# A ConvNeXt V2 block: PE drains replaced by waits, a narrower second read of yn, three more blocks stored whole, and reloads issued by SyncE

## The chip, the cores and the metric
The kernel runs on one core of one Trainium2 chip. The metric is device time in microseconds. Three runs of the kernel before took 1484.35, 1483.92 and 1483.01 us, a median of 1483.92. The engines are called PE (TensorE; PEld is its weight load), DVE (VectorE), ACT (ScalarE), POOL (GpSimd) and SP (SyncE, which here only issues transfers).

## The reference
The input x is one image of 512 x 512 pixels with 96 channels in bf16.

```python
out = sum of xp[:, i:i+H, j:j+W, :] * dw[i, j]      # 3 x 3 depthwise convolution
h = _layernorm(out, axis=-1)                        # over the 96 channels
h = gelu(einsum('bhwc,ce->bhwe', h, w1))            # 96 -> 384
gx = sqrt((h * h).sum(axis=(1, 2)) + 1e-6)          # over all pixels, one value per channel
nx = gx / (gx.mean(axis=-1) + 1e-6)
h = grn_gamma * (h * nx) + grn_beta + h
return x + einsum('bhwe,ec->bhwc', h, w2)           # 384 -> 96
```

The sum of squares over all pixels splits the work: no output can be made before every pixel has gone through the first product and gelu.

## The kernel before
The image is cut into 128 blocks of four rows (2048 pixels). A quad is 512 pixels of a block; a block has four. The program has two phases.

**Phase 1** makes the statistics, in slots of one block each (lines 831 to 955). A slot loads x (SP), transposes it (DVE, `turn_x`), convolves (PE, `conv_taps`, lines 462 to 504), takes the layer norm's moments, writes the normalized yn to memory and reads it again with channels on partitions (`stage_write`, `stage_read`), and for an older block runs the first product and gelu (`mlp_units`: nine ACT instructions that turn PSUM banks into g). Sums of squares of g are taken by DVE (`entry`, one statistics instruction of 512 columns per third of a quad) for as many quads as `cm_quads` says, and by PE (`gram_next`) for the rest. There are 14 slots without MLP: the ramp and a few after it; the last 14 blocks go through `mlp_tail`.

The convolution uses PE in row tiles: weights of 64 x 32, so that the upper 64 partitions (h = 0) and the lower 64 (h = 1) can work at once. It has three bursts of 24 matmuls; burst n gives the upper half bank n and the lower half bank n+1 (modulo 3). [...] 

**Phase 2** (lines 1003 to 1026) goes through the blocks in the order ORDER. For each block it needs g with channels on partitions, W2s (w2 with the statistics in it, made between the phases) and xb = x + bias. There are three kinds of block:
- *held* (5): g stayed in on-chip memory;
- *whole* (35, those with q % 10 in 0, 3, 7 below 114): g was stored in phase 1 in three pieces of 512 KB, one per slot (`store_next`), and is reloaded as `gl`, 1536 KB, into one of two buffers;
- *recomputed* (88): yn is read again (`ynT`, a ring of six buffers) and the first product and gelu are done again, quad by quad (`recompute`, `cm_unit`: three matmuls of 512 columns and one gelu of 1536). For three of them (KEPT) the last read of phase 1 is still there.

ORDER spreads held and whole blocks evenly among the recomputed ones. The schedule of the quads is written out: `pace` (line 371) issues recomputed quads between the four parts of a block's second product, evenly over phase 2 and at most five blocks ahead.

At each position n the loop loads what position n+5 needs (`load_rest`, line 284; `load_xr`, line 276, x for the residual, five buffers), lets POOL make xb of position n+2 (`stage_xb`, line 321, three buffers, each free when DVE has used it), runs the second product (`stage_mm2`, line 329: 48 matmuls of 96 columns into two PSUM banks, and four DVE instructions that add xb and write o_sb, four buffers) and stores the block before (`stage_out`, on SP).

For the order of work: up to position 7 the queues are used in program order (the wrapper `InOrder`); from position 8 on (FIRST = 8, line 1014) a scheduler orders each engine's instructions when the program is built, by when it thinks that they can start. Queues are in order on the chip: an instruction that waits holds back all behind it. POOL carries xr issues, gl issues and xb; SP carries ynT issues and stores.

The read of yn in phase 2 (line 295, `yn_rows`) takes 128 rows of 4 KB in one transfer: the 96 of block q and 32 of block q+1, which rows of zeros in w1p multiply.

Of the kernel before, what the change touches and what calls it, by code (L numbers as in the profile page):

```python
# [12 lines left out]
GR = 4  # L13
# [3 lines left out]
FILL = (6, 15)  # L17
BATCH = 4
NHELD = 5
WHOLE = (0, 3, 7)  # L20
NTAIL = 14
GRB = 3

# [33 lines left out]
def kernel(  # L57
# [13 lines left out]
    bf16 = x.dtype  # L71
    assert bf16 == mybir.dt.bfloat16

    B, H, W, C = x.shape
    E = w1.shape[1]
    assert B == 1 and dw.shape[0] == 3 and dw.shape[1] == 3
    assert C == 96 and E % 128 == 0 and W == 512
    NI = C // 32
    NCH = E // 128
    NG = W // 128  # L80
    NBLK = H // GR
# [5 lines left out]
    yn_dram = dram.tile([NBLK, C, GR * W], bf16, name="yn_dram")  # L87
    r_dram = dram.tile([NBLK, GR, W], bf16, name="r_dram")

    TAIL0 = NBLK - NTAIL  # L90
    HELD = [NBLK - 2 - 2 * i for i in range(NHELD)][::-1]
    KEPT = [NBLK - 5, NBLK - 3, NBLK - 1]
# [2 lines left out]
        return q in HELD  # L95

    def is_whole(q):
        return q < TAIL0 and q % 10 in WHOLE

    def cm_quads(q):  # L100
        if is_whole(q) or is_held(q):
            return NQ
        if q > HELD[0]:
            return 1
        return 2 if q >= NBLK - 16 or (q - 1) % 10 in WHOLE else 3

    whole = [q for q in range(NBLK) if is_whole(q)]
    g_dram = dram.tile([len(whole), 128, NQ * NCH * QW], bf16, name="g_dram")
# [10 lines left out]
    def quad_out(flat_ap):  # L119
        return flat_ap.rearrange("p (g r m) -> p g r m", r=GR, m=MB)  # L120

    def yn_src(q):
        return yn_dram[q].rearrange("c (r w) -> c r w", r=GR)

    def yn_rows(q):
        return yn_dram[q:q + 2].rearrange("q c (r w) -> (q c) r w", r=GR)[0:128]

    def yn_dst(q, r):
        return yn_dram[q].rearrange("(c i) (r w) -> r c i w", i=NI, r=GR)[r]

# [5 lines left out]
    dwx = consts.tile([9, NI, GR, 32], bf16, name="dwx")  # L136
    eye32 = consts.tile([128, 32], bf16, name="eye32")
    rowsel = consts.tile([128, GR], bf16, name="rowsel")
    w1_raw = consts.tile([C, E], bf16, name="w1_raw")
    w1p = consts.tile([128, E], bf16, name="w1p")  # L140
    Wq = consts.tile([128, NI, 3, GR, 32], bf16, name="Wq")
    w2_sb = consts.tile([128, NCH, C], bf16, name="w2_sb")
# [42 lines left out]
    with ExitStack() as p1:  # L185
# [98 lines left out]
        def load_rest(n, sq, pq):  # L284
            q = ORDER[n]
            v = grp.setdefault(q, {})
            if is_held(q):
                v["g"] = gs[q]
            elif is_whole(q):
                v["g"] = late.gl.tile([128, NQ, NCH, QW], bf16, name="gl")  # L290
                pq.dma_start(out=v["g"][:].rearrange("p t j w -> p (t j w)"), in_=g_dram[whole.index(q)])
            else:
                ynt = yn_ring[SLOTS[nth_made[q] % NYT]]
                if q not in KEPT:
                    sq.dma_start(out=ynt[:], in_=yn_rows(q))
                v["ynt"] = ynt

        def recompute(q, t):
            if t == 0:
                grp[q]["g"] = late.gr.tile([128, NQ, NCH, QW], bf16, name="gr")  # L300
            cm_unit(grp[q]["g"], grp[q]["ynt"], t)

        def cm_unit(g, ynt, t):
            U = banks3()
            for j in range(NCH):
                pe.matmul(quad_out(U[:, j, :]), lhsT=w1p[:, j * 128:(j + 1) * 128],
                          rhs=quad(ynt[:], t), start=True, stop=True)
            act.activation(out=g[:, t, :, :], in_=U, func=ACTF.Gelu_apprx_tanh)

# [116 lines left out]
        def setup_mlp():  # L426
            Us = banks(1)[:, 0, :]
            w1m, b2_ps = Us[:, :E], Us[:, E:E + C]
            pe.matmul(w1m, lhsT=cen[:], rhs=w1_raw[:], start=True, stop=True)
            for j in range(NCH):  # L430
                pe.matmul(b2_ps, lhsT=bet_bf[:, j:j + 1].to_broadcast([128, 128]), rhs=w2_sb[:, j, :],
                          start=(j == 0), stop=(j == NCH - 1))
            dve.scalar_tensor_tensor(out=w1p[:C, :], in0=w1m[:C], scalar=-1.0 / C, in1=w1_raw[:],
                                     op0=ALU.mult, op1=ALU.add)
            dve.tensor_copy(out=B2bc_f[:], in_=b2_ps)

        def setup_rest():
            dve.memset(ones_f[:], 1.0)
            dve.tensor_copy(out=gam[:], in_=gam_bf[:])

# [21 lines left out]
        def conv_taps(b, spare):  # L462
            if spare:
                Ua, Ub = banks(2), banks(1)
                Y = [Ua[:, 0, :], Ua[:, 1, :], Ub[:, 0, :]]
            else:
                Y = [Y3[:, i, :] for i in range(NI)]
            mms = []
            for n in range(3):
                mms.append([(h, j, (n + h) % NI, dx) for dx in (0, -1, 1) for j in range(GR) for h in range(2)])  # L470
            flat = [m for ms in mms for m in ms]
            first = {}
            last = {}
            for n, (h, j, i, dx) in enumerate(flat):
                first.setdefault((i, j), n)
                last[i, j] = n

            def burst(n, fence=True):
                k = sum(len(ms) for ms in mms[:n])
                for h, j, i, dx in mms[n]:  # L480
                    src = b + shift(h, j)
                    o0, o1 = max(0, -dx), W - max(0, dx)
                    pe.matmul(
                        Y[i][32 * j:32 * j + 32, o0:o1],
                        lhsT=Wq[64 * h:64 * h + 64, i, dx + 1, j, :],
                        rhs=x_rows(src, 64 * h, 64 * h + 64, i, MB * (1 + dx) + o0, o1 - o0)
                        if 0 <= src < NBLK else zrow[64 * h:64 * h + 64, o0:o1],
                        start=first[i, j] == k,
                        stop=last[i, j] == k,
                    )  # L490
                    k += 1
                if n < 2 and fence:
                    pe.drain()

            def evac():
                y = ypool.tile([128, NI, W], bf16, name="y_bf")
                if spare:
                    act.activation(out=y[:, 0:2, :], in_=Ua, func=ACTF.Identity)
                    act.activation(out=y[:, 2, :], in_=Ub[:, 0, :], func=ACTF.Identity)
                else:  # L500
                    act.activation(out=y[:], in_=Y3, func=ACTF.Identity)
                ybf[b] = y

            return [lambda fence=True, n=n: burst(n, fence) for n in range(3)], evac

        def stage_sq(b, on_act):
            q = ysqpool.tile([128, NI, W], bf16, name="ysq")
# [323 lines left out]
        for s in range(last_slot + 1):  # L831
# [30 lines left out]
            if mlp and mlp[0] >= TAIL0:  # L862
                assert not taps
                square_owed()
                mlp_tail(mlp[0], get)
            elif not mlp:
                if s + 3 < NBLK:
                    turn_x(s + 3)
                for f in taps:
                    f()  # L870
                if not spare:
                    spread_out()
                if evac:
                    evac()
                for b in get("sqa"):
                    stage_sq(b, True)
                for b in get("stats"):
                    stage_stats(b)
                for k in get("moments"):
                    stage_moments(k)  # L880
                if spare:
                    spread_out()
                for k in get("chain"):
                    stage_moments(k)
                    stage_chain(k)
                for k in get("turn"):
                    stage_turn(k)
                gram_next(2)
                square_owed()
            else:  # L890
                b = mlp[0]
                unit, squares, squares_rest = mlp_units(b)
                conv = lambda n, fence=True: taps[n](fence) if taps else None

                conv(0)
                unit(0, 2)
                unit(2, 1)
                squares(0)
                conv(1, False)
                spread_out()  # L900
                if s + 3 < NBLK:
                    turn_x(s + 3)
                unit(3, 1)
                unit(4, 2)
                squares(1)
                gram_next(1 if taps else 2)
                unit(6, 1)
                squares(2)
                unit(7, 1)
                for k in get("turn"):  # L910
                    stage_turn(k)
                conv(2)
                if evac:
                    evac()
                gram_next(1 if taps else 2)
                unit(8, 2)
                unit(10, 1)
                for b2 in get("stats"):
                    stage_stats(b2)
                unit(11, 1)  # L920
                for k in get("moments"):
                    stage_moments(k)
                squares_rest(2)
                square_owed()
                if is_whole(b):
                    owed.append(lambda f=squares_rest: f(3))
                grams.extend((b, c) for c in range(cm_quads(b) * QC, NQ * QC, 2 * E))
                if is_whole(b):
                    stores.extend((b, h) for h in range(3))
# [127 lines left out]
```

## Time and profile before

| | |
|---|---|
| runs, median | 1484.35, 1483.92, 1483.01 us; 1483.92 |
| span of the profiled execution | 1483.2 us (from the first to the last instruction; the page gives no other time for this execution, and the three runs take 0.2 us less to 1.1 us more than the span) |
| PE busy | 1392.2 us (94%) |
| ACT busy | 1415.9 us (95%) |
| POOL busy | 1300.7 us (88%) |
| DVE busy | 1166.9 us (79%) |
| bytes moved | 433.08 MB, 292 GB/s over the span; 410 to 415 in slices 31 to 35 of 40 |
| ACT g<-PS 128x1024, 128x512 | x342 of 1116 ns, x684 of 701 ns |
| ACT gr<-PS 128x1536 (recomputed) | x360 of 1455 ns |
| POOL xb<-xr 128x1536 | x118 of 3133 ns |
| POOL issues: xr, gl | 555 ns, 537 ns each |
| gl<-g_dram | x35, 1536 KB, 10.9 us from issue to landing |
| ynT<-yn_dram in phase 2 | x85, 512 KB each |
| out_dram<-o_sb | x127, 384 KB each |

A busy share is the time in which an engine has an instruction under way; successive instructions overlap a little, so a mean duration is longer than the distance between two starts, and distances between starts are what a bound engine is measured by. "Idle before, with a releaser" says what ended the wait of an engine. A store or load shows as the issuing instruction on its engine; its landing shows in the waits of others. `SPq` and `POOLq` are the issuing sides.

### The profile page before, as it was taken

What the parts mean: (1) busy time and instruction counts of PE and PEld (TensorE: products, weight loads), DVE (VectorE), ACT (ScalarE), POOL (GpSimd) and SP (SyncE); (2) the same over time, 40 slices, a digit from 0 to 9 for tenths busy, and PEclk for the clock granted to TensorE, in tenths of its full rate; (3) what the DMA queues carried; (4) which work ended last, traced back from release to release, by engine and by line L of the source; (5) the groups of instructions that cost most, each with busy time, mean ns of one, the idle gap of its engine ahead of it and who ended that gap; (6) DMA issues with size and microseconds to landing.
All of it is one profiled execution on the core that took longest, in us unless ns stands there. A gap on an engine that the chain in (4) does not pass through costs nothing.

```text
span 1483.2 us, 54230 instructions
## 1 busy us (share of the span) xinstructions
PE 1392.2 (94%) x23125; PEld 812.3 (55%) x23125; DVE 1166.9 (79%) x2139; ACT 1415.9 (95%) x1595; POOL 1300.7 (88%) x922
## 2 busy tenths in 40 slices
PE   8889999999999999999999997789999999999998
PEld 3334444444444444444444445467777777676766
DVE  7749989999999999999999987955555555555555
ACT  6889999999999999999999999989999999998997
POOL 3459889998999999999999996559999999999997
PEclk9999999999999999999999999999999999999999
DMA  6577788887878888888888867569999999999997
GB/s 178 166 215 235 231 245 282 250 267 243 276 240 274 258 266 259 276 248 280 265 248 264 260 217 210 188 248 404 366 352 410 415 414 413 415 408 410 401 406 279
DMA packets 167768, 433.08 MB, mean 292 GB/s; under 512 B 31558, under 2 KB 81318, under 8 KB 163046
## 3 DMA queue, kind: packets, MB, share of 16 engines
q1 hardware_dynamic: 151284, 326.04, 66.8%
q0 software_dynamic: 14880, 103.43, 17.6%
q8 instruction: 181, 2.97, 0.9%
q14 instruction: 61, 0.50, 0.1%
q10 hardware_dynamic: 1362, 0.15, 0.1%
HBM read 273.30 MB, written 156.22 MB: 290 GB/s over the span
## 4 chain that ended last, share of the span: by engine, by line
PE 31%; ACT 25%; DMA 20%; DVE 10%; POOL 8%; issue 4%; SPq 3%; ACTq 0%; POOLq 0%; DVEq 0%
PE PS L35 31%; ACT g L35 18%; DMA out_dram<-o_sb 9%; ACT y_bf L35 6%; DVE bst L35 5%; POOL yn L35 4%; DMA ynT<-yn_dram 4%; SPq L35 3%; DMA rbc<-r_dram 2%; DMA xin<-in_x_dram 2%; DVE xT L35 2%; DMA yn_dram<-yn 2%; POOL ysq L35 1%; DVE o_sb L35 1%; DMA g_dram<-g 1%
## 5 line engine op out<-in xcount | busy, mean ns | idle before, releaser
L35 ACT ACTIVATE g<-PS 128x512 bf16<-128x512 f32 (+2 forms) x1062 | 727.2, 862 | 9.3 <-PE PS L35 9.1
L35 DVE BATCH_NORM_STATS2 bst<-g 128x6 f32<-128x512 bf16 x1110 | 671.3, 673 | 29.3 <-ACT g L35 28.8
L35 PE MATMUL PS<-ynT,w1p 128*128 128x512 bf16 x2181 | 610.0, 381 | 24.2 <-ACT g L35 5.4
L35 ACT ACTIVATE gr<-PS 128x1536 bf16<-128x1536 f32 x360 | 498.9, 1455 | 27.2 <-PE PS L35 18.7
L35 DVE TENSOR_TENSOR o_sb<-PS,xb 128x384 bf16<-128x384 f32 x512 | 278.0, 557 | 231.2 <-PE PS L35 184.9
L35 POOL TENSOR_TENSOR yn<-y_bf,rbc 128x1536 bf16<-128x1536 bf16 x126 | 391.6, 3111 | 75.1 <-DMA rbc<-r_dram 23.5
L325 POOL TENSOR_TENSOR xb<-xr,B2c 128x1536 f32<-128x1536 bf16 x118 | 368.4, 3133 | 7.9 <-DVE o_sb L35 5.5
L35 PE MATMUL PS<-xT,Wq 64*32 64x511 bf16 (+1 forms) x9198 | 339.7, 388 | 27.5 <-ACT y_bf L35 7.7
L35 POOL TENSOR_TENSOR ysq<-y_bf 128x1536 bf16<-128x1536 bf16 x114 | 314.0, 2755 | 14.4 <-ACT y_bf L35 14.3
L35 PEld LDWEIGHTS <-w1p 128*128 128x128 bf16 x2181 | 171.4, 98 | 221.3 <-issue 130.4
L35 PEld LDWEIGHTS <-gr 128*128 128x128 bf16 x4296 | 213.1, 98 | 75.8 <-issue 19.7
L35 PE MATMUL PS<-W2s,gr 128*128 128x96 bf16 x4224 | 224.5, 206 | 13.8 <-DVE o_sb L35 13.4
L35 PEld LDWEIGHTS <-Wq 64*32 64x32 bf16 x9216 | 112.5, 90 | 192.9 <-issue 145.9
L35 ACT ACTIVATE y_bf<-PS 128x1536 bf16<-128x1536 f32 (+2 forms) x135 | 199.4, 1483 | 17.9 <-PE PS L35 13.3
L35 DVE STREAM_TRANSPOSE xT<-xin 128x576 f32<-128x576 f32 (+1 forms) x256 | 181.8, 750 | 13.1 <-DMA xin<-in_x_dram 11.0
L35 PEld LDWEIGHTS <-g 128*128 128x128 bf16 x1704 | 105.1, 98 | 89.1 <-issue 57.4
L35 PE MATMUL PS<-w1p,ynT 128*128 128x256 bf16 (+2 forms) x822 | 125.6, 273 | 7.7 <-ACT xT L35 3.2
L35 PE MATMUL PS<-g 128*128 128x128 bf16 x1464 | 122.9, 220 | 5.0 <-DVE PS L35 4.9
L35 PEld LDWEIGHTS <-gl 128*128 128x128 bf16 x1680 | 82.9, 98 | 24.4 <-issue 2.4
L35 PE MATMUL PS<-W2s,gl 128*128 128x96 bf16 x1680 | 89.6, 206 | 1.1 <-DVE o_sb L35 0.8
L35 PEld LDWEIGHTS <-ynT 128*128 128x128 bf16 x822 | 64.1, 98 | 31.1 <-issue 13.3
L280 POOL DMA_DIRECT2D xr<-in_x_dram x115 | 63.8, 555 | 14.2 <-POOL xb L325 14.2
(106 smaller groups left out, 559.9 us busy)
## 6 DMA issues: line engine op xcount, KB each, us to landing
xin<-in_x_dram SPq DMA_DIRECT2D x126, 432.0 KB
g_dram<-g SPq DMA_DIRECT2D x105, 512.0 KB
gl<-g_dram POOLq DMA_DIRECT2D x35, 1536.0 KB, 10.9
yn_dram<-yn SPq DMA_DIRECT2D x512, 96.0 KB
ynT<-yn_dram SPq DMA_DIRECT2D x128, 384.0 KB
out_dram<-o_sb SPq DMA_DIRECT2D x127, 384.0 KB
xr<-in_x_dram POOLq DMA_DIRECT2D x123, 384.0 KB, 6.9
ynT<-yn_dram SPq DMA_DIRECT2D x85, 512.0 KB
```

The costliest lines, as they stand in the source:

```text
L35: r = f(*a, **k)
L280: pq.dma_start(out=xr[:], in_=x[0, r0:r0 + GR].rearrange("r w c -> (r w) c").rearrange("(p g) c -> p g c", g=PXP))
L325: pq.tensor_tensor(out=xb[:], in0=grp[q]["xr"][:], in1=bias[:, None, :].to_broadcast([128, PXP, C]), op=ALU.add)
```

## The change
Four edits, and what goes with them:

1. `pe.drain()` is gone. At the first upper-half matmul into a bank whose lower half was written by the burst before, a `pe.nop()` waits for that burst's last matmul. It is there in all slots, before bursts 1 and 2.
2. The read of yn in phase 2 takes 96 rows, in three transfers of 32 rows that go to every fourth partition (i, i+4, ...). So the weights for it, `w1s`, have the rows of w1p at those partitions and zeros at every fourth one. w1s shares its memory with w1_raw, is zeroed by POOL in slot 4 and filled by three small transfers on SP. KEPT blocks still use w1p.
3. Every third block below 114 is whole: 38 instead of 35; 85 are recomputed instead of 88. `cm_quads` follows: 4, 2, 3 in turn.
4. SP (`sq`) issues the reloads gl, POOL (`pq`) keeps xr and xb.

```diff
-WHOLE = (0, 3, 7)
+EVERY = 3
...
-        return q < TAIL0 and q % 10 in WHOLE
+        return q < TAIL0 and q % EVERY == 0
...
-        return 2 if q >= NBLK - 16 or (q - 1) % 10 in WHOLE else 3
+        return 2 if q >= NBLK - 16 or q % EVERY == 1 else 3
...
-    w1_raw = consts.tile([C, E], bf16, name="w1_raw")
+    w1s = consts.tile([128, E], bf16, name="w1s")
+    w1_raw = w1s[:C]
...
-                pq.dma_start(out=v["g"][:].rearrange("p t j w -> p (t j w)"), in_=g_dram[whole.index(q)])
+                sq.dma_start(out=v["g"][:].rearrange("p t j w -> p (t j w)"), in_=g_dram[whole.index(q)])
...
-                    sq.dma_start(out=ynt[:], in_=yn_rows(q))
+                    for i in range(NI):
+                        sq.dma_start(out=ynt[i:128:4], in_=yn_src(q)[i:C:NI])
...
-            cm_unit(grp[q]["g"], grp[q]["ynt"], t)
+            cm_unit(grp[q]["g"], grp[q]["ynt"], t, w1p if q in KEPT else w1s)
...
         def setup_rest():
+            pool.memset(w1s[:], 0.0)
+            for i in range(NI):
+                sp.dma_start(out=w1s[i:128:4, :], in_=w1p[i:C:NI, :])
...
-                    pe.matmul(
+                    if h == 0 and (1, i) in done:
+                        tc.add_manual_dep(pe.nop().ins, done.pop((1, i)).ins.name,
+                                          mybir.DependencyInfo(mybir.DependencyClass.Sync, mybir.DependencyReason.DATA),
+                                          reason="row tiles of one bank")
+                    done[h, i] = pe.matmul(
...
-                if n < 2 and fence:
-                    pe.drain()
...
-                conv(1, False)
+                conv(1)
```

More of the change, by code (lines that the diff above doesn't have):

```diff
@@ L123, in yn_src @@
         return yn_dram[q].rearrange("c (r w) -> c r w", r=GR)
-    def yn_rows(q):
-        return yn_dram[q:q + 2].rearrange("q c (r w) -> (q c) r w", r=GR)[0:128]
     def yn_dst(q, r):
@@ L300, in recompute, with cm_unit @@
                 grp[q]["g"] = late.gr.tile([128, NQ, NCH, QW], bf16, name="gr")
-            cm_unit(grp[q]["g"], grp[q]["ynt"], t)
-        def cm_unit(g, ynt, t):
+            cm_unit(grp[q]["g"], grp[q]["ynt"], t, w1p if q in KEPT else w1s)
+        def cm_unit(g, ynt, t, wt=w1p):
             U = banks3()
             for j in range(NCH):
-                pe.matmul(quad_out(U[:, j, :]), lhsT=w1p[:, j * 128:(j + 1) * 128],
+                pe.matmul(quad_out(U[:, j, :]), lhsT=wt[:, j * 128:(j + 1) * 128],
                           rhs=quad(ynt[:], t), start=True, stop=True)
@@ L428, in setup_mlp @@
             w1m, b2_ps = Us[:, :E], Us[:, E:E + C]
-            pe.matmul(w1m, lhsT=cen[:], rhs=w1_raw[:], start=True, stop=True)
+            pe.matmul(w1m, lhsT=cen[:], rhs=w1_raw, start=True, stop=True)
             for j in range(NCH):
@@ L432, in setup_mlp @@
                           start=(j == 0), stop=(j == NCH - 1))
-            dve.scalar_tensor_tensor(out=w1p[:C, :], in0=w1m[:C], scalar=-1.0 / C, in1=w1_raw[:],
+            dve.scalar_tensor_tensor(out=w1p[:C, :], in0=w1m[:C], scalar=-1.0 / C, in1=w1_raw,
                                      op0=ALU.mult, op1=ALU.add)
@@ L476, in conv_taps, with burst @@
                 last[i, j] = n
-            def burst(n, fence=True):
+            done = {}
+            def burst(n):
                 k = sum(len(ms) for ms in mms[:n])
@@ L502, in evac @@
                 ybf[b] = y
-            return [lambda fence=True, n=n: burst(n, fence) for n in range(3)], evac
+            return [lambda n=n: burst(n) for n in range(3)], evac
         def stage_sq(b, on_act):
@@ L892 @@
                 unit, squares, squares_rest = mlp_units(b)
-                conv = lambda n, fence=True: taps[n](fence) if taps else None
+                conv = lambda n: taps[n]() if taps else None
                 conv(0)
```

## The prediction
> **What bounds the kernel now.** I read the page first (busy shares and slices), then busy time by stretch of time, then the waits and the time lines of the stretches that differ. The page's slices show two phases with a dip between them (about 950 to 980 us). By stretch (columns: stretch, length, then busy time and count of PE, PEld, DVE, ACT, POOL, granted clock, DMA share, GB/s):
>
> ```profile
> 500.00:550.00 50.00, 48.08 (x879) 23.58 (x864) 47.97 (x87) 50.00 (x73) 46.54 (x38) 1.00 0.88 275
> ...
> 1010.00:1470.00 460.00, 445.75 (x6490) 329.56 (x6488) 250.38 (x462) 439.46 (x318) 438.55 (x261) 1.00 1.01 399
> ```
>
> Phase 1 is bound by ACT: 50.00 of 50 us busy. Its time line shows y_bf starting every 7.05 us, one slot:
>
> ```profile
> 504.88 1.61 ACT L35 ACTIVATE y_bf<-PS 128x1536 bf16<-128x1536 f32 x1
> 506.22 5.97 ACT L35 ACTIVATE g<-PS 128x1024 bf16<-128x1024 f32 x9
> 511.96 1.56 ACT L35 ACTIVATE y_bf<-PS 128x1536 bf16<-128x1536 f32 x1
> ```
>
> Phase 2 is a near tie: PE 446 and ACT 439 of 460 us, the DMA share at 1.01, POOL 439. The waits of 1010 to 1470 us (columns: total us, times, longest) say which engine really never rests:
>
> ```profile
> DVE o_sb L35 <- DMA out_dram<-o_sb: 41.3, 30, 3.3
> ...
> POOL xr L280 <- POOL xb L325: 14.2, 48, 0.3
> ...
> POOL xb L325 <- DVE o_sb L35: 5.5, 7, 1.6
> DVE o_sb L35 <- POOL xb L325: 4.3, 6, 1.4
> ```
>
> POOL's 438.6 us busy and 14.2 us of waiting for **itself** (0.30 us each, an xr load that reuses the buffer which the xb just ahead of it read) and 5.5 us of waiting for DVE make 458 of 460 us. So POOL is at its pace; DVE's waits for stores (41.3 us) show DMA close behind it. POOL's time line shows the pace in two patterns. With reloads, three blocks take 1130.10 - 1118.28 = 11.82 us, 3.94 each:
>
> ```profile
> 1118.28 0.54 POOL L291 DMA_DIRECT2D gl<-g_dram  x1
> 1118.83 6.22 POOL L325 TENSOR_TENSOR xb<-xr,B2c 128x1536 f32<-128x1536 bf16 x2
> 1124.99 1.11 POOL L280 DMA_DIRECT2D xr<-in_x_dram  x2
> 1126.12 3.13 POOL L325 TENSOR_TENSOR xb<-xr,B2c 128x1536 f32<-128x1536 bf16 x1
> 1129.55 0.56 POOL L280 DMA_DIRECT2D xr<-in_x_dram  x1 [0.30 <-POOL xb L325]
> 1130.10 0.54 POOL L291 DMA_DIRECT2D gl<-g_dram  x1
> ```
>
> Without a reload, xb and xr alternate and each xr pays the 0.30 us: 1046.72 - 1042.70 = 4.02 us a block.
>
> ```profile
> 1042.70 3.14 POOL L325 TENSOR_TENSOR xb<-xr,B2c 128x1536 f32<-128x1536 bf16 x1
> 1046.15 0.56 POOL L280 DMA_DIRECT2D xr<-in_x_dram  x1 [0.30 <-POOL xb L325]
> 1046.72 3.15 POOL L325 TENSOR_TENSOR xb<-xr,B2c 128x1536 f32<-128x1536 bf16 x1
> ```
>
> That is the point of this case: every reload (0.54 us) is followed by a pair of xb and a pair of xr, and the pair spares one or two waits. After program position 8 of phase 2 the order on POOL is the scheduler's; it puts xr(n+5) behind xb(n), where its buffer comes free, unless xb(n+1) is already due, and it is due only after a reload has held POOL up.
>
> **Part 1, the drains.** In the weight loads' time line a conv burst (24 matmuls) that ends in a drain is followed 0.98 us after its start by the next load (67.69 -> 68.66, 68.66 -> 69.64), one that does not by 0.81 (69.64 -> 70.45): 0.17 us a drain. There are 114 slots with MLP and one drain, 14 without and two (ACT's ysq x14 counts them): 142 x 0.17 = 24 us of PE. The price of the nop that replaces them, a wait for the last matmul of the burst before, is shown by no row. In MLP slots whole units lie between the bursts, so the wait is over when PE gets there; where bursts adjoin (28 places) it lies between 0 and a drain's 0.17, or somewhat above if the signal travels slowly; I take 0.15, nearest to the drain, which waits for the same matmul. The 114 drains are hidden by ACT: from 200 to 850 us ACT is idle for some 2 us in all, so 19 us of PE buys at most that. The chain from 20 to 140 us has PE for 18% only. Gain: 0.5 us, bounds 5 and -2.
>
> The zeroing of w1s and its three small DMAs come in slot 4 on queues that then serve the first blocks; SP's small issues take 0.6 us there, so up to 1.8 us ahead of block 1's read (issued at 32.55, landing 4.5 us later, first used about 38). Mostly covered; I take 0.2. **Three more whole blocks** add nine stores of 512 KB to phase 1, one per slot where one slot in ten had none; the DMA share is 0.81 to 0.88 and ACT covers it. Quads with DVE statistics stay at 3.0 per block (30 per ten before, 4+2+3 per three after). Phase 1 together: -0.3 us, bounds -5 and +2.
>
> **Part 2, phase 2.** The other resources all get cheaper. PE: three quad matmuls take 0.65 us (1062.82 -> 1063.47), twelve W2s matmuls 0.51 (1063.47 -> 1063.98), so a block costs 4 x 0.51 = 2.05 and recomputing it 4 x 0.65 = 2.6: before, 7 of 10 recomputed, 3.87 a block; after, 2 of 3, 3.78. ACT: 1.40 a quad (15 in 21.07 us), 5.6 a recomputed block: 3.92 before, 3.74 after. DMA by the issue sizes: per ten blocks 10 x (384+384) + 3 x 1536 + 7 x 512 = 15872 KB before; per three 3 x 768 + 1536 + 2 x 384 = 4608 KB after. At 414 GB/s (slices 31 to 35 move 410 to 415) that is 3.93 and 3.80 us a block. POOL loses 35 reload issues (19 us by the rows), **but with them what made the pairs**: 3.10 + 0.30 + 0.56 + 0.06 = 4.02 at every block. So POOL's pace goes from 3.94 to 4.02 while all else falls to 3.8 or less, and POOL alone sets the end.
>
> The sum: xb of position 10 starts at 1005.32; with one reload issue fewer ahead of it at about 1004.9. 112 blocks at 4.02 put xb of position 122 at 1455.1, against 1453.25 now: +1.9 us. From there to the end takes 29.95 us now, since DVE lags two blocks behind POOL. Paced by POOL, DVE is level: 3.1 (xb) + 3.0 (rest of that block) + 3 x 3.78 + 2 x 2.75 (the last two, whose recomputation is done: 24 matmuls per 1.37 us at 1474 to 1479) + 2.9 (last store, as now) = 25.8: -4.1 us. Phase 2: -2.3 us, with phase 1 -2.6. The span is 1483.2, within the three timed runs (1483.01 to 1484.35); taken from their median, 1483.92 - 2.6 = 1481.3. A measurement of this kernel tells 0.2% (3 us) from no change, so the forecast lies just inside that.
>
> SP's queue: per three blocks it gains one reload and four more ynT issues, 5 x 0.33 = 1.7 us in 12; it waits 342 us for o_sb today, so issue time is covered. A reload waits for the W2s matmuls of the whole block two before; behind it on SP stand the next store and ynT loads, which would wait for much the same matmuls.
>
> The split read has no row in phase 2. The nearest is rbc in phase 1, four DMAs of 32 rows x 4 KB: 5.43 us from the last issue (332.66), like the 96-row read of 384 KB beside it (5.1 to 5.5). So I take no loss per byte; ends: 25% of the ynT time saved, or twice the time per byte (3.80 -> 4.43).
> [...]
> [...]
>
> **Rivals.** *POOL keeps pairs* (the scheduler finds xb due without a reload): POOL 3.66 a block, DMA at 3.80 binds, some 1% lost between the queues as now (3.99 against 3.94): 112 x 3.84 = 430 against 447.9, -18 us, less 0.4 and phase 1: about 1465. For it: pairs exist. Against: all stretches of up to six blocks without a reload (1034 to 1055, 1086 to 1102) alternate.
> *Stores behind reloads on SP's queue, slower*: a store now shares its queue with 1536 KB (3.8 us at 414 GB/s). Late stores land 12.5 to 15.6 us after DVE now; four o_sb buffers allow three blocks, 12.06 us, PE's two banks cover 1.9 more and PE's slack 3 x 0.24. Past 14.7 us each of some 36 reloads adds the excess: at 15.05, 36 x 0.35 = +13 us, 1494; at 15.6, +33, 1514. For it: DVE's 30 waits for stores. Against: 4608 KB per 12.06 us is 391 GB/s, 94% of 414, so queues should be shorter.
> *The drains were the limit in phase 1*: 19 us more, 1462. ACT's 50.00 of 50 us speaks against it.
>
> **How the numbers follow.** Forecast (1476 to 1486) 0.60; pairs 0.17 (with the little left for the drains); slower 0.23. The forecast lies 0.4 us inside the bound, so half of it falls on either side. Faster by over 0.2%: 0.17 + 0.31 = 0.48; within 0.2%: 0.29; slower: 0.23. The range 1464 to 1494 leaves out about half of each rival.
>
> **What would show it.** Right: POOL alternating at 4.02 us, the xr wait on xb near 115 x 0.30 = 34 us, DVE's waits for xb up from 4.3 to over 20 us and for stores well below 41; ACT's slot still 7.05; adjoining bursts 0.95 us apart. Wrong: pairs of xb without reloads, DVE waiting for stores more than 41 us, or y_bf starts under 7.0 us apart.

## The result, and the profile after

The kernel after takes 1497.62 us (median of 14 runs, 1485.69 to 1513.54), the kernel before, beside it, 1483.49 (14 runs). The ratio is 1.0077, 95% interval 1.0055 to 1.0099: slower by 0.8%. The forecast was 1481.3 and a range of 1464 to 1494. The profiled execution after took 1497.9 us, with a span of 1496.1.

Phase 1 is bound as was forecast. By stretch of time, columns as before (stretch, length, busy time and count of PE, PEld, DVE, ACT, POOL, clock, DMA share, GB/s), the kernel after:

```profile
500.00:550.00 50.00, 48.76 (x883) 23.90 (x867) 48.60 (x88) 50.00 (x72) 46.51 (x39) 1.00 0.86 273
1010.00:1470.00 460.00, 432.58 (x6282) 320.95 (x6279) 241.65 (x449) 416.07 (x299) 409.12 (x223) 0.99 1.00 372
```

ACT is still busy for 50.00 of 50 us, and y_bf starts 7.03 us apart (503.28 to 510.31; 7.05 by the prediction). In phase 2 **every** engine does less in the same time: PE 433 instead of 446 us, ACT 416 instead of 439, POOL 409 instead of 439, and 372 GB/s instead of 399, at the same full DMA share. Nobody works at its limit, so somebody waits. (The granted clock, 0.99 for 1.00, is not what holds it: PE is idle for 27 us here, where it was idle for 14.) POOL's time line first, after:

```profile
1037.31 3.13 POOL L324 TENSOR_TENSOR xb<-xr,B2c 128x1536 f32<-128x1536 bf16 x1
1040.73 0.55 POOL L278 DMA_DIRECT2D xr<-in_x_dram  x1 [0.30 <-POOL xb L324]
1041.31 3.13 POOL L324 TENSOR_TENSOR xb<-xr,B2c 128x1536 f32<-128x1536 bf16 x1
```

It alternates, 4.00 us a block (1041.31 - 1037.31), as forecast. But xb of position 122 starts at 1469.44, not at 1455.1. The waits from 1010 to 1470 us (total us, times, longest) say that POOL is held up from outside, by DVE, and DVE by stores:

```profile
DVE o_sb L35 <- DMA out_dram<-o_sb: 47.6, 21, 4.2
...
POOL xr L278 <- POOL xb L324: 32.7, 110, 0.3
...
DVE o_sb L35 <- POOL xb L324: 17.5, 18, 1.6
POOL xb L324 <- DVE o_sb L35: 13.1, 9, 3.1
POOL xr L278 <- issue: 2.9, 1, 2.9
```

From position 10 to 122 it takes 464.2 us: 13.1 of waiting for DVE, 2.9 of one pause with no releaser, and the rest is 112 x 4.00 of POOL's own pace. Why are stores late, when fewer bytes are moved? The waits of the **issuing** queue, SP, are a view of their own. Before, 1010 to 1470 us:

```profile
SPq L353 <- DVE o_sb L35: 290.2, 115, 5.9
SPq L295 <- PE PS L35: 90.8, 73, 3.5
```

SP waited for computing alone: for an o_sb to store, and for a ynT buffer to come free. After:

```profile
SPq L294 <- DMA gl<-g_dram: 154.9, 34, 6.6
SPq L352 <- DVE o_sb L35: 37.0, 56, 3.1
SPq L352 <- DMA out_dram<-o_sb: 36.2, 35, 2.5
```

34 times, 4.6 us each, SP does not **issue a read of yn** (line 294) until a **reload has landed**, although the two have no data in common. SP's time line after, one period (start, duration):

```profile
1189.40 0.38 SPq L289 DMA_DIRECT2D gl<-g_dram  x1
1189.87 0.48 SPq L352 DMA_DIRECT2D out_dram<-o_sb  x1
1190.40 2.46 SPq L294 DMA_DIRECT2D ynT<-yn_dram  x3
1192.96 0.53 SPq L352 DMA_DIRECT2D out_dram<-o_sb  x1
1193.53 6.82 SPq L294 DMA_DIRECT2D ynT<-yn_dram  x3
1201.14 0.34 SPq L352 DMA_DIRECT2D out_dram<-o_sb  x1
1201.58 0.38 SPq L289 DMA_DIRECT2D gl<-g_dram  x1
```

Count from the reload at 1189.40: a store (1), three pieces (2 to 4), a store (5), three pieces (6 to 8). The second group takes 6.82 us instead of 2.46, since its last piece, the eighth transfer after the reload, waits for the reload. Behind it stand a store (1201.14) and the next reload (1201.58), so stores come bunched and reloads 12.2 us apart here. This period is no exception: from 1010 to 1470 us SP's waits show 112 for a landing (34 for reloads, 54 for stores, 24 for reads of yn), and in the trace all 112 end with the landing of the transfer that SP issued eight before, whether it shares data with the waiting one or not. What makes SP wait for it the trace does not show; "the count" below stands for this distance of eight. Before, from 1010 to 1470 us, SP issued 189 transfers, some five per three blocks, none of them a reload, and no wait of SP was for a landing.

In phase 1, where SP issues more transfers, the kernel before had such waits already. SP's waits over the whole execution before have this line:

```profile
SPq L35 <- DMA ynT<-yn_dram: 11.6, 18, 1.7
```

All 18 are issues of rbc, which is read from r_dram and has no data in common with ynT, and all 18 end with the landing of the transfer eight before. So the trace of before showed that an issue can wait for an unrelated landing.

### The profile page after: what moved, and what is told of

Its sections match the earlier page's. It is cut to its first block, busy times and chain, and to the rows that moved or that the text cites. A ratio compares the mean times of both kernels' runs of the same rounds, so it can differ in the third digit from the quotient of the medians.

```text
span 1496.1 us, 54236 instructions
## 1 busy us (share of the span) xinstructions
PE 1394.2 (93%) x23104; PEld 816.7 (55%) x23104; DVE 1163.4 (78%) x2136; ACT 1404.4 (94%) x1583; POOL 1284.6 (86%) x888
## 4 chain that ended last, share of the span: by engine, by line
DMA 30%; PE 19%; ACT 16%; POOL 15%; DVE 10%; SPq 5%; issue 4%; POOLq 0%; DVEq 0%; ACTq 0%
PE PS L35 19%; DMA out_dram<-o_sb 15%; ACT g L35 11%; POOL yn L35 7%; DMA ynT<-yn_dram 6%; DVE bst L35 5%; SPq L35 4%; ACT y_bf L35 4%; DMA yn_dram<-yn 3%; DMA rbc<-r_dram 3%; POOL xb L324 2%; POOL ysq L35 2%; DMA xin<-in_x_dram 2%; POOL nt L35 2%; DVE xT L35 2%
## 5 line engine op out<-in xcount | busy, mean ns | idle before, releaser
L35 ACT ACTIVATE gr<-PS 128x1536 bf16<-128x1536 f32 x348 | 486.0, 1453 | 51.7 <-PE PS L35 41.6
L324 POOL TENSOR_TENSOR xb<-xr,B2c 128x1536 f32<-128x1536 bf16 x118 | 369.6, 3133 | 15.4 <-DVE o_sb L35 13.1
L35 PE MATMUL PS<-ynT,w1p 128*128 128x512 bf16 x1158 | 338.8, 382 | 17.6 <-ACT g L35 5.4
L35 PE MATMUL PS<-ynT,w1s 128*128 128x512 bf16 x984 | 269.4, 383 | 0.1
L35 PEld LDWEIGHTS <-gr 128*128 128x128 bf16 x4152 | 208.4, 99 | 88.1 <-issue 36.6
L35 PE MATMUL PS<-W2s,gr 128*128 128x96 bf16 x4080 | 219.7, 208 | 27.9 <-DVE o_sb L35 27.7
L35 ACT ACTIVATE y_bf<-PS 128x1536 bf16<-128x1536 f32 (+2 forms) x135 | 202.4, 1504 | 15.3 <-PE PS L35 10.6
L35 PEld LDWEIGHTS <-w1p 128*128 128x128 bf16 x1158 | 95.2, 97 | 168.4 <-issue 122.3
L35 PEld LDWEIGHTS <-gl 128*128 128x128 bf16 x1824 | 89.2, 98 | 24.7 <-issue 1.5
L35 PEld LDWEIGHTS <-w1s 128*128 128x128 bf16 x984 | 78.7, 98 | 39.9 <-issue 2.0
L35 PE MATMUL PS<-W2s,gl 128*128 128x96 bf16 x1824 | 95.9, 207 | 0.8 <-DVE o_sb L35 0.7
```

The costliest lines, as they stand in the source:

```text
L35: r = f(*a, **k)
L324: pq.tensor_tensor(out=xb[:], in0=grp[q]["xr"][:], in1=bias[:, None, :].to_broadcast([128, PXP, C]), op=ALU.add)
```

## The experiments

**Theories.** *Count*: the three-piece read (with the reload ten SP transfers per three blocks, six if reads are in one piece) and the reload on SP (10.9 us from issue to landing in the kernel before, where POOL issued it) are harmless alone; together they make SP wait for landings, and stores and reloads queue behind that wait. *Queue*: the reload on SP is enough, stores stand behind 1536 KB (the prediction's slower rival). *Split*: narrow pieces are enough, they move more slowly. The first four expectations were written before the count was seen and name only the other two.

All ratios are to the kernel before in the same job (medians there 1489.0, 1488.7 and 1489.6 us; for after, 1483.5). Phase 1 ends (xb of position 3) between 977.8 and 991.1 us in these profiles, also where its instructions are the same. So the table gives the rest by itself: from xb of position 3 to the end, and in it positions 10 to 122; then SP's waits for reloads to land and DVE's waits for stores, 1010 to 1465 us. The ratios rest on 6 to 14 executions of a kernel, the columns behind them on the profiled one alone. That one lies 9 us under the median for a_tiny, 9 over it for a_one96, 7 over it for c_two_in, and within 3 for the others. Differences of a few us in these columns are therefore not shown: b_gl_sp is slower by its ratio, and its phase 2 is no longer than before's.

| kernel | read of yn | reloads on | ratio [95%] | phase 2, us | 10 to 122 | SP for gl | DVE for out |
|---|---|---|---|---|---|---|---|
| before | 1 x 128 rows | POOL | 1 | 504.7 | 447.9 | 0 | 41.3 |
| after | 3 x 32 | SP | 1.0077 [1.0055, 1.0099] | 518.3 | 464.2 | 154.9 | 46.3 |
| b_split | 3 x 32 | POOL | 0.9958 [0.9932, 0.9984] | 496.1 | 443.4 | 0 | 2.2 |
| b_gl_sp | 1 x 128 | SP | 1.0029 [1.0011, 1.0048] | 504.3 | 451.5 | 1.0 | 17.8 |
| a_gl_pool | 3 x 32 | POOL | 0.9964 [0.9944, 0.9983] | 497.7 | 444.4 | 0 | 0.7 |
| a_wide | 1 x 128 | SP | 1.0007 [0.9989, 1.0025] | 507.4 | 453.2 | 5.8 | 51.9 |
| a_13 | 1 x 128 | POOL | 1.0006 [0.9984, 1.0029] | 505.1 | 448.4 | 0 | 49.0 |
| a_tiny | 1 x 128, 2 x 4 bytes | SP | 1.0097 [1.0064, 1.0130] | 512.9 | 457.5 | 58.0 | 49.2 |
| a_one96 | 1 x 96 | SP | 1.0164 [1.0116, 1.0212] | 531.0 | 471.3 | 11.0 | 57.0 |
| a_gl_act | 3 x 32 | ACT | 1.0046 [1.0018, 1.0073] | 508.6 | 453.6 | 64.9 | 19.1 |
| a_two8 | 64 + 32 | SP | 1.0027 [0.9999, 1.0055] | 506.7 | 451.6 | 30.8 | 1.4 |
| a_inorder | 3 x 32 | SP | 1.0137 [1.0100, 1.0175] | 521.3 | 462.3 | 145.4 | 63.8 |
| c_two_in | 64 + 32 | SP | 0.9929 [0.9904, 0.9954] | 499.9 | 440.2 | 84.8 | 30.9 |
| c_xr_sp | 3 x 32 | POOL | 1.0173 [1.0136, 1.0209] | 530.7 | 471.8 | 0 | 67.9 |

### One edit taken back, one edit alone

Four kernels: the change with the reloads on POOL again (a_gl_pool), the change with the 128-row read again (a_wide), and the kernel before with only the reloads moved (b_gl_sp) or only the read split (b_split).

```diff
 a_gl_pool, against after
-                sq.dma_start(out=v["g"][:].rearrange("p t j w -> p (t j w)"), in_=g_dram[whole.index(q)])
+                pq.dma_start(out=v["g"][:].rearrange("p t j w -> p (t j w)"), in_=g_dram[whole.index(q)])
 a_wide, against after (and w1p for all blocks)
-                    for i in range(NI):
-                        sq.dma_start(out=ynt[i:128:4], in_=yn_src(q)[i:C:NI])
+                    sq.dma_start(out=ynt[:], in_=yn_rows(q))
```

b_gl_sp and b_split make the same two edits the other way round in the kernel before.

> The changed kernel with one edit undone: GpSimd issues the reloads of stored g again. Queue theory (with the reloads on SyncE's queue nearly all bytes stand in one queue and the DMA engines, always busy, move 375 instead of 414 GB/s): about 410 GB/s again between 1010 and 1470 us, waits of DVE for stores under 30 us, time 1470 to 1482. Split theory (the reads in pieces of 32 rows cost the rate): rate stays at 370 to 385 GB/s, waits for stores over 40 us, time 1490 to 1500. Either way GpSimd should show pairs of xb after reloads again.

> The changed kernel with the second read of yn as before: one transfer of 128 rows, 512 KB, weights w1p. Split theory: the rate is back at 405 to 415 GB/s although there are 7% more bytes, GpSimd alternates at 4.02 us a block and sets the end, 1478 to 1484. Queue theory: rate stays near 375 GB/s and the bytes are more, so 1505 to 1520.

> The kernel before with one edit alone: SyncE issues the reloads. Queue theory: the rate between 1010 and 1470 us falls from 399 to about 370 GB/s and the time rises by 20 to 35 us, since the bytes are still those of before. Split theory: the rate stays over 395; GpSimd alternates at 4.02 us a block, so the time moves by less than 5 us.

> The kernel before with one edit alone: the second read of yn takes 96 rows in three transfers of 32 rows. Queue theory: 7% fewer bytes at 414 GB/s free the DMA engines, GpSimd's 3.95 us a block is left as the bound, waits of DVE for stores fall from 41 to under 15 us, 1472 to 1481. Split theory: the rate falls to about 375 GB/s and the time rises by 5 to 15 us.

Measured: 0.9964, 1.0007, 1.0029, 0.9958. The times in these expectations go by a kernel before of some 1484 us, which took 1489.0 beside these runs. Neither theory came out whole. The rates from 1010 to 1465 us are 390, 404, 402 and 385 GB/s: the two 128-row reads move at the split theory's rate, or nearly, and yet b_split, the split alone, is the faster one, which the queue theory had said. Neither the queue nor the split makes the loss alone. Phase 2 changes by -8.6 us from the split and by -0.4 from the moved reloads, but by +13.6 with both (and the other two edits, which a_13 below puts at +0.4): some 22 us come from the **combination**. The split, with its fewer bytes, is even a gain: DVE's waits for stores fall from 41.3 to 2.2 us. POOL sets the pace in a_gl_pool, and DVE waits for it, 1010 to 1465 us:

```profile
DVE o_sb L35 <- POOL xb L324: 72.1, 68, 4.0
...
POOL xr L278 <- POOL xb L324: 12.5, 42, 0.3
```

With the reloads on POOL its waits for itself are down to 12.5 us: the pairs are back. In b_split SP also waits for landings, of stores (55.0 us at line 352 and 32.1 at line 294), and loses nothing by it; so not every such wait hurts. Those come to 2.3 us per three blocks, the ones for reloads after to 4.6 at one place.

### The count without the split: two 4-byte transfers

```diff
 a_tiny, against a_wide
                     sq.dma_start(out=ynt[:], in_=yn_rows(q))
+                    for i in range(2):
+                        k = 2 * nth_made[q] + i
+                        sq.dma_start(out=tiny[:, 2 * k:2 * k + 2], in_=yn_src(q)[0:1, 0, 0:2])
```

> The changed kernel with the single 128-row read of yn again (no split), and two transfers of 4 bytes each added behind each such read, on SyncE's queue: ten transfers per three blocks as in the changed kernel, in the same order, but nothing split. The 4-byte transfers fetch nothing that is used. COUNT THEORY (SyncE does not issue the eighth transfer after a reload until that reload of 1536 KB, some 11 us, has landed, and with ten transfers per three blocks that eighth one comes within the same three blocks, ahead of a store): SyncE waits over 100 us for reloads between 1010 and 1465 us, DVE's waits for xb over 10 us, time 1.004 to 1.010 of before, like the changed kernel (1.0077). SPLIT THEORY (the narrow pieces of 32 rows are what the queue loses time on): SyncE waits under 15 us for reloads, time as with the single read alone, 0.999 to 1.003 of before.

Measured: 1.0097, where a_wide had 1.0007: the loss is back with nothing split and 8 bytes more per read. SP's waits, 1010 to 1465 us:

```profile
SPq L299 <- DMA gl<-g_dram: 52.8, 20, 3.5
SPq L357 <- DMA ynT<-yn_dram: 41.9, 34, 2.0
SPq L357 <- DMA out_dram<-o_sb: 32.7, 30, 1.9
```

A 4-byte transfer (line 299) waits for the reload, 52.8 us in all, and with other lines SP waits 58.0 us for reloads, not the 100 that the count theory said; waits for other landings, 41.9 and 32.7 us, stand beside it. The profiled execution (1494.23 us) is one of the fastest of its 11 (1492.53 to 1512.90), so the usual one may wait longer. The ratio is as expected, the wait's share of it is not, and what such a small transfer costs by itself is not separated here.

### The bytes without the count: one transfer of 96 rows

```diff
 a_one96, against after (and w1p for all blocks)
-                    for i in range(NI):
-                        sq.dma_start(out=ynt[i:128:4], in_=yn_src(q)[i:C:NI])
+                    sq.dma_start(out=ynt[:C], in_=yn_src(q))
```

> The changed kernel with yn's 96 rows read by one transfer to partitions 0 to 95, in place of three transfers spread over all partitions: as few bytes as in the changed kernel, six SyncE transfers per three blocks. COUNT THEORY: SyncE waits under 15 us for reloads between 1010 and 1465 us; time like the 128-row read in the changed kernel (1.0007 of before) or up to 0.2% less for the bytes, 0.998 to 1.002. SPLIT THEORY (fewer bytes per partition row, 96 rows, are what costs): at or above 1.004.

Measured: 1.0164, a miss for the count theory; the split theory's number (1.004 or more) came out, though b_split, with as few rows, is faster than before and not slower. SP's waits are like those of a_wide (268.6 us for DVE, 11.0 for reloads; there 264.2 and 5.8), so the count is harmless, as said. But 384 KB to partitions 0 to 95 is slower than 512 KB to all 128, with 365 GB/s at a DMA share of 1.01 where a_wide has 404. So the narrow read gains in spread pieces (b_split) and loses in one piece on 96 partitions; whether the spread or the number of pieces makes the difference was not separated. The cause of the loss against a_wide (1.0164 for 1.0007) stays open.

### The reloads on ACT

```diff
 a_gl_act, against after
-                sq.dma_start(out=v["g"][:].rearrange("p t j w -> p (t j w)"), in_=g_dram[whole.index(q)])
+                (act if sq is sp else nc.scalar).dma_start(out=v["g"][:].rearrange("p t j w -> p (t j w)"), in_=g_dram[whole.index(q)])
```

> The changed kernel with the reloads of stored g issued by ScalarE in place of SyncE; three-piece reads stay. COUNT THEORY: the wait comes from a count that SyncE keeps of what it has outstanding; if the count takes in the transfers of ScalarE too, SyncE still waits over 100 us for reloads and the time stays at 1.004 to 1.010 of before; if each engine has its own, SyncE's wait for reloads is zero and the time falls to 0.994 to 0.999. SAME-QUEUE THEORY (stores are late because they stand behind 1536 KB in one queue, whoever waits): no wait of SyncE for reloads and 0.994 to 0.999. [...]

Measured: 1.0046. SP, which issues no reload any more, still waits for them:

```profile
SPq L294 <- DMA gl<-g_dram: 61.2, 27, 3.9
...
SPq L352 <- DMA gl<-g_dram: 3.7, 1, 3.7
```

The eight are counted over both engines: from the reload that ACT issues at 1192.44 us, SP issues a store (1193.09), two pieces (from 1194.59), a store (1196.29), two pieces (from 1196.68) and a store (1200.45), and the next piece, the eighth transfer, starts at 1203.02, 10.6 us after the reload; two xr loads that POOL issues in between (1196.13, 1200.13) are not in the count. After the reloads at 1180.49 and 1204.19 the eighth starts at 1191.90 and 1215.14, 11.4 and 11.0 us later. The waits are shorter than after (64.9 against 154.9 us) and so is the loss; my 100 us was too much. A wait of SP for a transfer of another queue cannot come from SP's queue being full: against the queue theory.

### Eight transfers per three blocks instead of ten

```diff
 a_two8, against after (w1s is filled to match)
-                    for i in range(NI):
-                        sq.dma_start(out=ynt[i:128:4], in_=yn_src(q)[i:C:NI])
+                    sq.dma_start(out=ynt[0:128:2], in_=yn_src(q)[0:64])
+                    sq.dma_start(out=ynt[1:128:4], in_=yn_src(q)[64:96])
```

> The changed kernel with yn's 96 rows read in two transfers (64 rows to every second partition, 32 rows to every fourth) in place of three: the same bytes, still spread over all partitions, reloads still on SyncE, but eight SyncE transfers per three blocks in place of ten, so the eighth after a reload comes only with the next reload, some 12 us later. COUNT THEORY: SyncE's waits for reloads to land fall from 155 us to under 30 between 1010 and 1465 us, DVE's waits for stores from 46 to under 25, and GpSimd's 4.02 us a block sets the end: 0.993 to 0.999 of before. SPLIT THEORY (loss in proportion to the pieces): two of three parts of the loss stay, 1.003 to 1.006.

The same bytes to the same partitions, reloads on SP, two issues fewer per three blocks. SP's waits, then DVE's, 1010 to 1465 us:

```profile
SPq L352 <- DVE o_sb L35: 192.8, 108, 3.8
SPq L289 <- PE PS L35: 62.2, 31, 3.0
SPq L289 <- DMA gl<-g_dram: 30.3, 24, 2.7
```

```profile
DVE o_sb L35 <- POOL xb L324: 109.8, 92, 3.6
...
DVE o_sb L35 <- DMA out_dram<-o_sb: 1.4, 1, 1.4
```

No read waits for a reload any more; the 30 us left are nearly all on line 289, the next reload, which also waits for a buffer that PE must free (62.2 us). DVE's waits for stores fall from 46.3 to 1.4 us, and DVE waits for POOL. Reloads start 12.1 us apart on the average (30 of them from 1110 to 1470 us), 12.6 after (29): POOL's 3 x 4.0 against SP's own round of landing, last piece, store, reload. Positions 10 to 122 take 451.6 us, where the prediction's model of POOL said 450.2. The ratio, 1.0027 [0.9999, 1.0055], is above what I expected (0.993 to 0.999): two thirds of the loss are gone, but the time does not fall below that of before.

This divides the 22 us of the combination. Phase 2 is 11.6 us shorter than after (506.7 for 518.3): by these profiles, that is the count. It is still 9.0 us longer than in a_gl_pool (497.7), where the reloads are on POOL; 7.2 of these lie between positions 10 and 122. Without its one pause of 2.9 us POOL takes 4.01 us a block there, alternating, and 3.94 in a_gl_pool, with pairs. These are the prediction's own two paces (4.02 and 3.94). So some half of the combination is not the count: once the split has taken DVE's waits for stores away, POOL without its pairs costs its full price. The ratios (0.9964, 1.0027, 1.0077) divide it in much the same way. (The number of pieces differs too between these two kernels, two and three.)

### POOL held to program order, with three pieces and with two

```diff
 a_inorder against after, c_two_in against a_two8
-            sq, pq = (sp, pool) if n < FIRST else (nc.sync, nc.gpsimd)
+            sq, pq = sp if n < FIRST else nc.sync, pool
```

In program order an xr load stands one xb later than the scheduler puts it, and its 0.30 us wait goes.

> The changed kernel with GpSimd held to program order in all of phase 2, so that an xr load stands behind the xb two blocks after the one that frees its buffer: its wait of 0.30 us per block should go, and GpSimd should need 3.72 us a block in place of 4.02. COUNT THEORY (the late stores behind SyncE's wait for reloads set the end, not GpSimd's pace): no gain over the changed kernel, 1.004 to 1.010 of before, GpSimd waiting for DVE in place of itself. GPSIMD THEORY (its 4.02 us a block sets the end): 112 times up to 0.2 us are gained, 0.988 to 0.996.

> Both of the above: two transfers per read, and GpSimd in program order. COUNT THEORY with the transfers as the next limit at 414 GB/s (4608 KB per three blocks, 3.80 us a block): 112 blocks gain 0.15 to 0.2 us each against the two-transfer version, 0.980 to 0.988 of before. RIVAL (reads of 96 spread rows cannot be moved faster than the 371 to 390 GB/s at full share seen so far, 4.03 us a block at 390): no gain over the two-transfer version, 0.993 to 0.999 or above.

a_inorder: 1.0137, no gain, as the count theory said, but above its 1.004 to 1.010 (why there is a loss against after was not followed up). POOL's wait for itself is gone from the list, and nothing came of it:

```profile
DVE o_sb L35 <- DMA out_dram<-o_sb: 63.8, 30, 4.2
POOL xb L35 <- DVE o_sb L35: 52.5, 58, 4.5
```

POOL now waits for DVE (52.5 us) and DVE for stores. So POOL's pace is not what ends the kernel after; with SP's wait at 145.4 us nothing faster on POOL can help.

c_two_in: 0.9929 [0.9904, 0.9954], the lowest ratio of all, 0.7% under the kernel before. The same edit is worth some 1% once SP does not hold the stores. That is the edge of what the rival said, and short of the 0.980 to 0.988 of the count theory. POOL needs 3.68 us a block where nothing holds it (xb at 1202.09 and 1205.77), but SP has the next limit:

```profile
SPq L352 <- DVE o_sb L35: 133.1, 86, 3.6
SPq L289 <- DMA gl<-g_dram: 83.8, 28, 4.7
```

The eighth transfer after a reload is the next reload, and now that one waits for its landing. Whether the count or the transfers (389 GB/s) is the limit there was not tried.

### More transfers on SP, none of them large

```diff
 c_xr_sp, against a_gl_pool
-                load_xr(n + PRE, pq)
+                load_xr(n + PRE, sq)
```

> The changed kernel with the reloads back on GpSimd and, in phase 2, the loads of xr issued by SyncE in place of GpSimd. GpSimd then has 3.1 us a block and 0.54 us per reload, 3.3 us a block, in place of 3.94. COUNT THEORY: no transfer over 384 KB stands in SyncE's order, so no long wait there, and the end is set by the transfers (3.80 to 3.85 us a block) or ScalarE: 112 blocks gain 0.1 us each over the version with the reloads on GpSimd alone (0.9964): 0.985 to 0.990 of before. RIVAL: an xr load waits on SyncE for GpSimd's addition and holds up the store behind it, or thirteen issues per three blocks wait for one another: DVE's waits for stores over 40 us and 0.996 to 1.005.

Measured: 1.0173; the improvement that I hoped for has the highest ratio of all (a_one96, 1.0164, cannot be told from it). POOL has only 357 us of work in 455, and SP, 1010 to 1465 us:

```profile
SPq L294 <- DMA out_dram<-o_sb: 86.5, 67, 5.4
SPq L352 <- DMA xr<-in_x_dram: 76.6, 25, 4.7
```

SP has twelve transfers of 128 or 384 KB per three blocks, so the eighth comes after some 8 us (8/12 of 12). In the kernel before xr took 6.8 us to land, in the kernel after 7.1 (medians, 1010 to 1470 us, issued by POOL). That is no margin: SP waits for stores and xr to land, and no reload is needed for it. The rival said so (waits over 40 us, 0.996 to 1.005), with too low a price.

### The other two edits alone

a_13 is a_wide with the reloads on POOL: drains gone and 38 blocks whole, nothing else.

> The drains and the number of whole blocks alone: the changed kernel with the single 128-row read and the reloads on GpSimd again. By the prediction's terms: phase 1 at most 0.5 us shorter, GpSimd's pairs at 3.94 us a block as before with three reload issues more: 0.997 to 1.001 of before. RIVAL (the three more stored blocks or the new waits of TensorE cost): above 1.002.

Measured: 1.0006 [0.9984, 1.0029]: neither edit can be told from nothing. The kernel with 142 drains less is no faster.

## Why the prediction was wrong

**The drains: right.** ACT hides them (a_13). Where bursts adjoin they start 0.97 us apart after (65.44 and 66.41 in the weight loads' time line), 0.98 before: the nop costs nearly a drain, 0.16 of 0.17 us. The rival of 1462 us is out.

**POOL: right in mechanism and size.** It alternates, at 4.00 us (forecast 4.02), its waits for itself are 32.7 us (34), and there are no pairs of xb while xr loads last. Where nothing else holds it, a_two8, the middle has 451.6 us (450.2). The tail has 26.7 us after (25.8). The rival in which POOL keeps pairs is out. What losing the pairs costs was booked at 1.9 us in the middle, against a kernel before that was also held up by late stores; against a_gl_pool, where they are not late, it is 7.2.

**The split read: right, and undervalued.** No loss per byte was taken; alone it even gives 0.9958. The prediction held POOL's pace to be the limit before and saw nothing to win from fewer bytes. But with fewer bytes DVE's 41.3 us of waits for stores went, and 8.6 us of phase 2 with them. In b_split the three pieces gain 0.42%, with a quarter fewer bytes in the read, so what they pay for being three is less than the bytes save. What that price is by itself no run separates; with the reloads on SP their number cost, by the count.

**The step that failed is SP's queue**: "it waits 342 us for o_sb today, so issue time is covered". Issue time was covered (342 us is the whole execution; 290.2 of them lie between 1010 and 1470). What was not looked at is that an issue can itself wait, for the landing of a transfer eight back (112 such waits after, 1010 to 1470 us). Four more ynT issues were priced at 4 x 0.33 us; they brought 154.9 us of waits into SP's queue, and 464.2 - 451.6 = 12.6 us between positions 10 and 122, by the difference to a_two8. POOL's nine waits for DVE, 13.1 us, make up that difference; a_two8 has none. In phase 2 the forecast was -2.3 us and after has +13.6: of these 15.9 us, 11.6 are after against a_two8, and 4.3 are in a_two8 too.

**The slower rival had the sign, the place and nearly the price** (1494; stores late, DVE waiting for them over 41 us, a few tenths of a us per reload), with the wrong mechanism: sharing a queue with 1536 KB. b_gl_sp and a_two8 have that and DVE's waits for stores fall, to 17.8 and 1.4 us; a_wide has it too, and its 51.9 us are much like the 49.0 of a_13, which has the reloads on POOL; a_gl_act does not have it and SP still waits. What was put against it, 391 GB/s of 414, was no argument: from 1010 to 1465 us after moved 371 GB/s, and a_two8, with the same bytes to the same places, 384; what was short after was the issuing.

Left open: a_two8 is not faster than before, by 1.0027 [0.9999, 1.0055] against a forecast of 0.998. Its phase 2 is 4.3 us longer than the sum: 1.0 before position 10, 1.4 in the middle (where POOL has one pause of 2.9 us) and 1.8 in the tail (27.6 us for 25.8). Why, and how much of it is scatter, stays open; so do the prices within a_tiny.

## What to carry to other kernels

Count the transfers that an issuing engine has under way at once, not only their bytes and issue times: here all 112 of SP's waits for a landing (after, 1010 to 1470 us) were for the transfer eight places back, with ACT's transfers in the count where ACT issued the reloads (a_gl_act), and a reload of 1536 KB among many short transfers stalled the queue behind it (154.9 us in 34 waits). When an edit cuts one transfer into several, look up which transfer now stands at the distance that the waits show, and read the issuing queue's own waits: a wait for the landing of a transfer whose data the waiting one does not touch is the mark, and the kernel before may show it in another phase. Two edits that are each free can meet in such a shared count, so they are to be tried together as well as apart.

## What was not expected of the hardware

- **A DMA share near 1 did not tell the kernels apart.** It is 0.99 to 1.01 from 1010 to 1465 us in all fourteen profiles, with rates between 364 GB/s (c_xr_sp, stores late) and 406 (a_13); a_two8 has 1.00 at 384 GB/s, and its stores are hardly waited for (1.4 us).
- **96 rows are not 96 rows.** Spread over all partitions (b_split, three pieces) they are faster than 128 rows, 0.9958; on partitions 0 to 95 in one piece (a_one96 against a_wide) slower, 1.0164 against 1.0007. Two spread pieces with the reloads on SP, as in a_one96, are at 1.0027 (a_two8). Placement and number of pieces were not separated.
